# A SwiGLU kernel's first loads in another order: gates of F tiles 2 and 3 ahead of x 256-511, and one F tile of the next tokens run by halves

## The chip, the core and the metric

The kernel runs on one core of a Trainium2 chip. The metric is device time in microseconds (us) of one execution; the kernel before took 115.84 us (median of three runs, 115.55 to 115.91). The engines are named as in the profile: PE is the matrix engine (PEld its weight loads), DVE the vector engine, ACT the scalar engine, POOL the GpSimd engine, and SP the engine that here only issues DMA transfers. The 16 DMA engines move what SP and ACT issue.

## What is computed

```python
B, S, D, F = 1, 2048, 512, 1376          # x: [1, S, D], all bf16

def reference(x, w_gate, w_up, w_down):
    g = _silu(x @ w_gate)
    u = x @ w_up
    return (g * u) @ w_down
```

With S = 2048 tokens, the gate and up products have an inner dimension of 512 (four blocks of 128) and 1376 columns: ten F tiles of 128 and a rest of 96.

## The kernel before

**Tiles and stages.** Tokens are taken in four chunks of 512 (c = 0 to 3; 'tokens 512-1023' are chunk 1), F in tiles of 128 (ft = 0 to 9). Two F tiles make a unit u. A plain gate or up group of one F tile and one chunk is 4 inner blocks of 512 tokens, each a pair of matmuls of 64 weight columns that stand side by side in the array and run together (`gu_emit`, L424); a group of whole chunks is thus 4 pairs. Most units are not done plainly, but by a seven-product scheme (class `Unit`, L610 and L622) on 2 chunks by 2 F tiles, which needs sums of weight blocks (`w_sums`, on POOL, written to ss_sb) and of token blocks (`x_sums`, written to tt_sb: T1 to T4). Ahead of these units, F tiles 0 to 3 of chunk 0 and the first three tiles of `early` (0, 1, 2) of chunk 1 are done plainly. After all of that the down projection runs (L720, L748, L858, L870), again with a seven-product scheme in part.

**The front.** x is needed transposed (inner dimension on the partitions). Tokens 0 to 255 come as plain rows (`xn`) and are transposed on PE (L373, L380); tokens 256 to 511 (`x0b`), 512 to 767 (`x1a`), 768 to 1023 (`x1b`) and later chunks come through transposing DMAs (L279). Weights come in slabs of two F tiles, gate and up apart (L267): `wg0` and `wu0` hold F tiles 0 and 1, `wg2` and `wu2` F tiles 2 and 3. PE starts with matmuls on constants (L350), transposes xn, and then runs, each as soon as its load has landed: the gates of F tiles 0 and 1 on tokens 0-255 (matmuls of 256 columns), the same gates on tokens 256-511, the ups of F tiles 0 and 1, then gates and ups of F tiles 2 and 3 (`classic(0, [2, 3])`, L1012), then `classic(1, [ft])` for F tiles 0, 1, 2 of chunk 1 (L1013). Each finished pair of groups goes through `classic_out`: a silu on ACT (L332) and a product on DVE (L337).

**What sets the order.** All work is recorded in a `Plan`. PE and SP keep the order in which the code records it; ACT, DVE and POOL are ordered by a small list scheduler from durations, lags, priorities and expected landing times written in the code. Each recorded operation waits only on semaphores of what it needs. SP issues the loads one after another into one queue that all 16 DMA engines serve; a load's semaphore counts 16 when all of them have finished their part. The load semaphores named below are s_dma30 = wg0, s_dma22 = x0b, s_dma21 = wu0, s_dma29 = wg2, s_dma20 = wu2, s_dma0 = x1a, s_dma1 = x1b; s_A, s_D, s_G and s_P count finished operations of ACT, DVE, POOL and PE.

**PSUM banks.** Groups take the 8 banks in turn (0, 2, 1, 3, 4, 5, 6, 7). In chunk 0 the first four groups use banks 0 to 3, the next four 4 to 7.

**Two chains beside PE.** The token sums T1 to T4 of chunks 0 and 1 are made on DVE and wait for x1a, x1b and the weight sums of unit 0 on POOL (which need wg0 and wu0). The weight sums of the next units on POOL wait for the last of T1 to T4.

Of the kernel before, what the change touches and what calls it, by code (L numbers as in the profile page):

```python
# [168 lines left out]
def bass_standalone__swiglu_ffn__prompt_kernel(nc, x, w_gate, w_up, w_down, out):  # L169
    _, S, D = x.shape  # L170
    F = w_gate.shape[1]
    P = 128
    KD = D // P
# [4 lines left out]
    SC = 512  # L178
# [6 lines left out]
    HT = SC // 2  # L185
    HC = P // 2
    NXN = HT // P
    NB = 8
# [10 lines left out]
    with ExitStack() as es:  # L199
# [55 lines left out]
        def load(name, emit, writes, busy, lag):  # L255
            nonlocal landed
            landed += lag
            i = take(homes[name] if name in homes else rest[0])
            plan.add("S", emit, writes=writes, busy=busy, lag=1800, dma=(i, 16)).land = landed + (300 if landed < 10000 else 1600)

        slabs = [(0, 2), (2, 4), (4, 6), (6, 8), (8, NFF + 1)]
        slab_of = {ft: a for a, b in slabs for ft in range(a, b)}

        def load_w(name, src, m, c0, f0, f1):
            load(
                name,
                lambda e: e.dma_start(  # L267
                    w_sb[:, :, m, c0:c0 + f1 - f0], src[:, f0:f1].rearrange("(k p) f -> p k f", p=P)
                ),
                [name], 600, 3.7 * (f1 - f0),  # L270
            )

        def load_slab(a, b):
            load_w(f"wg{a}", w_gate, 0, a * P, a * P, min(b * P, F))
            load_w(f"wu{a}", w_up, 1, a * P, a * P, min(b * P, F - 32))

        def load_x(name, t0, t1):
            load(
                name, lambda e: e.dma_start_transpose(xT_sb[:, :, t0:t1], xf[t0:t1, :]), [name], 1500, 4 * (t1 - t0)  # L279
            )  # L280
# [5 lines left out]
            ),  # L286
            ["xn"], 500, 770,
        )
        load_w("wg0", w_gate, 0, 0, 0, slabs[0][1] * P)
        load_x("x0b", HT, SC)  # L290
        load_w("wu0", w_up, 1, 0, 0, slabs[0][1] * P)
        load_slab(*slabs[1])
        for i in range(2):
            load_x(f"x1{'ab'[i]}", SC + i * HT, SC + (i + 1) * HT)
        load_slab(*slabs[2])
# [18 lines left out]
        for i in range(2):  # L314
            load(
                f"wdy{i}",
                lambda e, i=i: e.dma_start(wdt_sb[2 * R * i:2 * R * (i + 1), 0, :], w_down[NFF * P:F - R, :]),
# [12 lines left out]
        def silu_op(out, src, reads, writes, prio=5, busy=A_BUSY):  # L330
            return plan.add(
                "A", lambda e: e.activation(out, src, ACT.Silu), reads, writes, busy, A_LAG, prio  # L332
            )

        def tt_op(engs, out, a, b, alu, reads, writes, prio, busy, after=()):
            return plan.add(
                engs, lambda e: e.tensor_tensor(out, a, b, alu), reads, writes, busy,  # L337
                G_LAG if engs == "G" else D_LAG, prio, after=after,
            )
# [5 lines left out]
        def pe(emit, reads, writes, n, step=PE_STEP, after=()):  # L345
            return plan.add("P", emit, reads, writes, int(n * step), PE_LAG, dma=None, after=after)
# [58 lines left out]
        n_group = 0  # L405

        def next_bank():
            nonlocal n_group
            b = turn[n_group % NB]
            n_group += 1  # L410
            return b

        def x_keys(c):
            if c == 1:
                return ["x1a", "x1b"]
            if c:
                return [f"x{c}"]
            return [("x0a", dk) for dk in range(KD)] + ["x0b"]

        def gu_emit(m, ft, c, b, dks, n0, n1):  # L420
            def emit(e):
                for dk in dks:
                    for h in (0, HC):
                        ins = e.matmul(  # L424
                            psum[h:h + HC, b, n0:n1], lhsT=w_sb[:, dk, m, ft * P + h:ft * P + h + HC],
                            rhs=xT_sb[:, dk, c * SC + n0:c * SC + n1], start=(dk == 0), stop=(dk == KD - 1),
                            tile_position=(0, h),
                        )
                return ins
            return emit  # L430

        def gu_whole(m, ft, c, b):
            def emit(e):
                for dk in range(KD):
                    ins = e.matmul(  # L435
                        bank(b), lhsT=w_sb[:, dk, m, ft * P:(ft + 1) * P], rhs=xT_sb[:, dk, c * SC:(c + 1) * SC],
                        start=(dk == 0), stop=(dk == KD - 1),
                    )
                return ins
            return emit  # L440

        def gu_group(m, ft, c, b, whole=False):
            emit = gu_whole(m, ft, c, b) if whole else gu_emit(m, ft, c, b, range(KD), 0, SC)
            pe(emit, x_keys(c) + [f"w{'gu'[m]}{slab_of[ft]}"], [("b", b)], KD)
# [3 lines left out]
        def ring(name, tiles):  # L448
            n = rings.get(name, 0)
            rings[name] = n + 1  # L450
            i = n % len(tiles)
            return tiles[i][:, :], (name, i)

        def hview(ft, c):
            return (h0_sb, h1_sb)[c // 2][:, ft, c % 2 * SC:(c % 2 + 1) * SC]
# [8 lines left out]
        def classic_out(ft, c, bg, bu):  # L464
            sg, ksg = ring("sg", sg_sb)
            silu_op(sg, bank(bg), [("b", bg)], [ksg])
            tt_op("D", hview(ft, c), sg, bank(bu), ALU.mult, [ksg, ("b", bu)], [("h", ft, c)], 5, D_BUSY)

        def classic(c, fts, own=None):
            gates = [next_bank() for ft in fts] if own is None else own[:1]  # L470
            ups = [next_bank() for ft in fts] if own is None else own[1:]
            for ft, b in zip(fts, gates):
                gu_group(0, ft, c, b, own is not None)
            for ft, b in zip(fts, ups):
                gu_group(1, ft, c, b, own is not None)
            for ft, bg, bu in zip(fts, gates, ups):
                classic_out(ft, c, bg, bu)
# [91 lines left out]
        def x_sums(pi, eng, prio, after):  # L569

            c0, c1 = 2 * pi, 2 * pi + 1
            xk = x_keys(c0) + x_keys(c1)
            key = lambda n, k: ("tt", pi, X_SUM[n], k)
            last, first = after, None
            for n in ("T1", "T2", "T3", "T4"):
                behind = last
                last = []
                for k0, k1 in [(0, KH)] if pi == 0 else [(k, k + 1) for k in range(KH)]:
                    block = lambda k, c: xT_sb[:, k * KH + k0:k * KH + k1, c * SC:(c + 1) * SC]
                    at = lambda n: tt_sb[pi][:, X_SUM[n], k0:k1, :]  # L580
                    rd = lambda n: at(n).bitcast(FP32)
                    B11, B12, B21, B22 = (block(k, c) for k in range(2) for c in (c0, c1))
                    a, b, of_ = {
                        "T1": (B12, B11, ()), "T2": (B22, rd("T1"), ["T1"]),
                        "T3": (B22, B12, ()), "T4": (B21, rd("T2"), ["T2"]),
                    }[n]
                    last.append(tt_op(
                        eng, at(n), a, b, ALU.subtract, xk + [key(o, k) for o in of_ for k in range(k0, k1)],
                        [key(n, k) for k in range(k0, k1)], prio, 1160 if eng == "D" else 1250, behind,
                    ))  # L590
                first = first or last
            for k in range(KH):
                cast_op("A", tt_sb[pi][:, X_SUM["B22"], k, :], xT_sb[:, KH + k, c1 * SC:(c1 + 1) * SC], xk, [key("B22", k)], 8, A_BUSY, first if pi else ())
            return last
# [89 lines left out]
                silu_op(sg, g, [kg], [ksg], 3)  # L684
                tt_op("G", hview(ft, c), sg, v, ALU.mult, [ksg, kv], [("h", ft, c)], 3, 1250, h_free(ft, c))

        g0, u0, g1, u1 = [next_bank() for i in range(4)]
        wkey = [f"wg{slab_of[0]}", f"wu{slab_of[0]}"]
        for dk in range(KD):
            for ft, b in ((0, g0), (1, g1)):  # L690
                pe(gu_emit(0, ft, 0, b, [dk], 0, HT), [("x0a", dk), wkey[0]], [("b", b)], 0.5)
        for ft, b in ((0, g0), (1, g1)):
            pe(gu_emit(0, ft, 0, b, range(KD), HT, SC), ["x0b", wkey[0]], [("b", b)], 2)
        for ft, b in ((0, u0), (1, u1)):
            gu_group(1, ft, 0, b)
        classic_out(0, 0, g0, u0)
        classic_out(1, 0, g1, u1)

        F_ORDER = [ft for u in U_ORDER[1] for ft in (2 * u, 2 * u + 1)]
        LAST_T = NST - 1  # L700
# [308 lines left out]
        units = [(pi, u) for pi in range(2) for u in U_ORDER[pi]]  # L1009
        early = [2 * u + i for u in range(NFF // 2) if u not in U_ORDER[0] for i in range(2)]  # L1010
        sums = w_sums(0, 8, (), "A")
        classic(0, [2, 3])  # L1012
        for ft in early[:3]:  # L1013
            classic(1, [ft])
        sums = x_sums(0, "D", 6, sums)
        for u in U_ORDER[0]:
            sums = w_sums(u, 2, sums, "A")
        sums = x_sums(1, "G", 2, sums)
# [68 lines left out]
```

## Time and profile before

| what | before |
|---|---|
| median of three runs | 115.84 us (115.55 to 115.91) |
| profiled execution, its own time | 115.91 us |
| its span, first to last instruction | 114.6 us |
| PE busy | 110.9 us (97%) |
| DVE, ACT, POOL busy | 76.8, 63.8, 61.5 us |
| granted PE clock | 1.000 |
| HBM read, written | 4.75 MB, 2.10 MB |

The span is the time from the first to the last instruction; the 1.3 us between it and the execution's own time lie outside the program. Matmuls overlap in the array, so a busy PE says little about its pace: the pace is read from the starts of two matmuls. The chain of work that ended last is followed back from the last instruction to what released each step; 'SPq' in it is SP's issuing of a DMA. In a timeline, each row begins with the start and the length in us, and brackets hold the idle time before it and what ended it. In the DMA view a load's row ends with the us from its issue to its landing.

### The profile page before, as it was taken

Reading aid. Unit: us, or ns where it says so; the run is one execution under the profiler, and the core shown is the slowest. Engines: PE = TensorE matmul, PEld = TensorE weight load, DVE = VectorE, ACT = ScalarE, POOL = GpSimd, SP = SyncE. Lnnn points to the kernel's source line nnn. Section 1 sums busy time; section 2 is a strip of 40 time slices with the busy share of each in tenths; the row PEclk is TensorE's granted clock in tenths of the full one; section 3 lists DMA queues with packets and bytes.
Section 4 is the critical chain, followed back from the end, with each engine's and each line's share of the span. In section 5 each row is a group of like instructions: output and inputs, shape, how many; then the busy total and the mean of one; then the engine's idle time right before and its main releaser. Section 6 shows DMA issues by size and latency. Waiting matters only on the chain.

```text
span 114.6 us, 1775 instructions
## 1 busy us (share of the span) xinstructions
PE 110.9 (97%) x652; PEld 70.4 (61%) x660; DVE 76.8 (67%) x113; ACT 63.8 (56%) x123; POOL 61.5 (54%) x57
## 2 busy tenths in 40 slices
PE   7999999999999999999999999999999999999993
PEld 2776566646685857677675858654344556866452
DVE  0113899874866839493957769499999957486423
ACT  5344565874878897767678786740576960000000
POOL 1059003999999999987999999975000000000000
PEclk9999999999999999999999999999999999999999
DMA  2998999995000000000000000000041002227966
GB/s 82 239 273 185 276 259 231 265 361 140 1 0 0 3 0 3 0 0 6 0 0 0 3 0 0 0 0 0 8 135 46 0 0 46 52 46 182 201 195 199
DMA packets 22808, 9.84 MB, mean 86 GB/s; under 512 B 12848, under 2 KB 22672, under 8 KB 22800
## 3 DMA queue, kind: packets, MB, share of 16 engines
q1 hardware_dynamic: 20656, 8.69, 31.6%
q10 hardware_dynamic: 2144, 1.05, 3.2%
q8 instruction: 5, 0.08, 0.3%
q14 instruction: 3, 0.02, 0.1%
HBM read 4.75 MB, written 2.10 MB: 60 GB/s over the span
## 4 chain that ended last, share of the span: by engine, by line
PE 86%; SPq 6%; DMA 4%; issue 1%; DVE 1%
PE psum L610 32%; PE psum L720 15%; PE psum L622 12%; PE psum L858 10%; PE psum L424 5%; DMA xT_sb<-in_x_dram 4%; PE psum L870 4%; SPq L279 4%; PE psum L488 3%; PE psum L748 3%; SPq L267 2%; PE psum L435 2%; PE psum L514 2%; DVE o_sb L326 1%; SPq L284 0%
## 5 line engine op out<-in xcount | busy, mean ns | idle before, releaser
L610 PE MATMUL psum<-tt_sb,ss_sb 128*128 128x512 f32 x160 | 40.0, 402 | 0.0
L610 PEld LDWEIGHTS psum<-tt_sb,ss_sb 128*128 128x128 f32 x160 | 29.9, 188 | 7.5 <-DVE psum L326 0.3
L337 DVE TENSOR_TENSOR ts_sb<-r_sb,psum 128x512 f32<-128x512 f32 x32 | 20.6, 682 | 14.7 <-ACT r_sb L325 14.7
L337 POOL TENSOR_TENSOR h_sb<-sg_sb,ts_sb 128x512 bf16<-128x512 f32 x16 | 20.8, 1302 | 2.8 <-ACT sg_sb L332 2.8
L337 DVE TENSOR_TENSOR h_sb<-sg_sb,psum 128x512 bf16<-128x512 f32 x24 | 16.4, 683 | 6.2 <-PE psum L424 5.8
L325 ACT ACTIVATE r_sb<-psum 128x512 f32<-128x512 f32 x32 | 17.3, 596 | 5.4 <-PE psum L610 5.4
L332 ACT ACTIVATE sg_sb<-psum 128x512 f32<-128x512 f32 x24 | 14.4, 602 | 10.6 <-PE psum L610 5.3
L337 POOL TENSOR_TENSOR ss_sb<-w_sb 128x512 fp32r<-128x512 bf16 x10 | 11.4, 1160 | 13.8 <-DVE tt_sb L337 7.5
L720 PE MATMUL psum<-wd_sb,h_sb 128*128 128x512 bf16 (+2 forms) x98 | 17.9, 336 | 0.2 <-issue 0.2
L622 PE MATMUL psum<-xT_sb,w_sb 128*128 128x512 bf16 x59 | 14.2, 380 | 0.4 <-issue 0.2
L720 PEld LDWEIGHTS psum<-wd_sb,h_sb 128*128 128x128 bf16 x100 | 8.3, 98 | 9.2 <-issue 1.0
L424 PE MATMUL psum<-xT_sb,w_sb 128*64 128x512 bf16 (+1 forms) x128 | 12.9, 362 | 0.2 <-DMA xT_sb<-in_x_dram 0.2
L332 ACT ACTIVATE sg_sb<-ts_sb 128x512 f32<-128x512 f32 x16 | 10.2, 637 | 2.2 <-DVE ts_sb L337 2.2
L424 PEld LDWEIGHTS psum<-xT_sb,w_sb 128*64 128x64 bf16 x128 | 8.4, 114 | 4.3 <-issue 0.7
L622 PEld LDWEIGHTS psum<-xT_sb,w_sb 128*128 128x128 bf16 x64 | 5.5, 98 | 7.9 <-issue 2.5
L326 DVE COPY psum<-psum 128x512 f32<-128x512 f32 x8 | 5.6, 699 | 0.8 <-PE psum L622 0.2
L337 POOL TENSOR_TENSOR ss_sb<-w_sb,ss_sb 128x512 fp32r<-128x512 bf16 x5 | 5.8, 1168 | 0.2
L337 POOL TENSOR_TENSOR ss_sb<-ss_sb,w_sb 128x512 fp32r<-128x512 f32 x5 | 5.8, 1166 | 0.0
L326 DVE CAST o_sb<-psum 128x512 bf16<-128x512 f32 (+2 forms) x6 | 3.0, 512 | 4.2 <-PE psum L720 3.1
L337 POOL TENSOR_TENSOR ss_sb<-wd_sb 128x640 fp32r<-128x640 bf16 x4 | 5.6, 1414 | 0.0
L858 PE MATMUL psum<-tt_sb,ss_sb 128*128 128x512 f32 x20 | 5.6, 418 | 0.0
L858 PE MATMUL psum<-th_sb,ss_sb 128*128 128x512 f32 x20 | 5.5, 411 | 0.0
(72 smaller groups left out, 122.4 us busy)
## 6 DMA issues: line engine op xcount, KB each, us to landing
wd_sb<-in_w_down_dram SPq DMA_DIRECT2D x1, 1280.0 KB, 8.1
w_sb<-in_w_gate_dram SPq DMA_DIRECT2D x4, 256.0 KB, 4.2
w_sb<-in_w_up_dram SPq DMA_DIRECT2D x4, 256.0 KB, 4.3
out_dram<-o_sb SPq DMA_DIRECT2D x7, 128.0 KB, 1.8
out_dram<-xT_sb ACTq DMA_DIRECT2D x4, 128.0 KB, 2.3
out_dram<-xT_sb ACTq DMA_DIRECT2D x2, 256.0 KB, 3.2
w_sb<-in_w_gate_dram SPq DMA_DIRECT2D x1, 352.0 KB, 5.0
w_sb<-in_w_up_dram SPq DMA_DIRECT2D x1, 320.0 KB, 4.3
```

The source lines that it names most:

```text
L279: name, lambda e: e.dma_start_transpose(xT_sb[:, :, t0:t1], xf[t0:t1, :]), [name], 1500, 4 * (t1 - t0)
L325: return e.activation(out, src, ACT.Copy)
L326: return e.tensor_copy(out, src)
L332: "A", lambda e: e.activation(out, src, ACT.Silu), reads, writes, busy, A_LAG, prio
L337: engs, lambda e: e.tensor_tensor(out, a, b, alu), reads, writes, busy,
L424: ins = e.matmul(psum[h:h + HC, b, n0:n1], lhsT=w_sb[:, dk, m, ft * P + h:ft * P + h + HC], rhs=xT_sb[:, dk, c * SC + n0:c * SC + n1], sta ...
L488: ins = e.matmul(psum[m:m + HC, b, :], lhsT=w_sb[:, dk, 0, XC0 + m:XC0 + m + HC], rhs=xT_sb[:, dk, c * SC:(c + 1) * SC], start=(dk == 0), ...
L610: ins = e.matmul(bank(dst), lhsT=s[:, k, :], rhs=t[:, k, :], start=(start and k == 0), stop=(k == KH - 1), skip_group_check=True,)
L622: ins = e.matmul(bank(dst), lhsT=w_sb[:, k0 + k, m, f:f + P], rhs=xT_sb[:, k0 + k, c:c + SC], start=(start and k == 0), stop=(k == KH - 1) ...
L720: ins = e.matmul(psum[:, b, 0:c1 - c0], lhsT=hrows(F_ORDER[n], t, 0, P), rhs=wd_sb[:, F_ORDER[n], c0:c1], start=(start and n == n0), stop= ...
L858: ins = e.matmul(bank(dst), lhsT=self.ds[s][:, j, self.q, :], rhs=self.dt[t][:, j, :], start=(start and n == 0), stop=(n == NFF // 2 - 1), ...
L870: ins = e.matmul(bank(dst), lhsT=wd_sb[:, 2 * j + a, d * P:(d + 1) * P], rhs=h0_sb[:, 2 * j + a, 0:SC], start=(n == 0), stop=(n == NFF // ...
```

## The change

Three things are moved; nothing is computed that was not computed before.

- **Loads.** wg2 is issued right behind wg0, ahead of x0b. The order is xn, wg0, wg2, x0b, wu0, wu2, x1a, x1b, and the same as before from there on.
- **Chunk 0.** Gates of F tiles 0 and 1 on tokens 0-255 as before; then gates of F tiles 2 and 3 on tokens 0-255; then the four gates on tokens 256-511; then the four ups on whole chunks, each followed by its silu and product. Gates take banks 0 to 3, ups 4 to 7. `classic(0, [2, 3])` falls away.
- **Chunk 1.** The first of its three plain F tiles (F tile 0) runs gate and up on tokens 512-767 (needs x1a alone), then both on tokens 768-1023 (needs x1b). The other two are unchanged.

The priority of `x_sums(0, ...)` is 4 instead of 6. In the order that the scheduler makes, all four products of chunk 0 stand ahead of T1 on DVE now, and T2 directly behind T1; before, the fourth product stood between them.

```diff
--- before.py
+++ after.py
@@ -286,10 +286,11 @@
             ),
             ["xn"], 500, 770,
         )
-        load_w("wg0", w_gate, 0, 0, 0, slabs[0][1] * P)
+        for a, b in slabs[:2]:
+            load_w(f"wg{a}", w_gate, 0, a * P, a * P, b * P)
         load_x("x0b", HT, SC)
-        load_w("wu0", w_up, 1, 0, 0, slabs[0][1] * P)
-        load_slab(*slabs[1])
+        for a, b in slabs[:2]:
+            load_w(f"wu{a}", w_up, 1, a * P, a * P, b * P)
         for i in range(2):
             load_x(f"x1{'ab'[i]}", SC + i * HT, SC + (i + 1) * HT)
         load_slab(*slabs[2])
@@ -684,17 +685,20 @@
                 silu_op(sg, g, [kg], [ksg], 3)
                 tt_op("G", hview(ft, c), sg, v, ALU.mult, [ksg, kv], [("h", ft, c)], 3, 1250, h_free(ft, c))
 
-        g0, u0, g1, u1 = [next_bank() for i in range(4)]
-        wkey = [f"wg{slab_of[0]}", f"wu{slab_of[0]}"]
+        first = range(4)
+        gates = [(0, 1, 2, 3)[ft] for ft in first]
+        ups = [NB // 2 + ft for ft in first]
+        n_group = NB
         for dk in range(KD):
-            for ft, b in ((0, g0), (1, g1)):
-                pe(gu_emit(0, ft, 0, b, [dk], 0, HT), [("x0a", dk), wkey[0]], [("b", b)], 0.5)
-        for ft, b in ((0, g0), (1, g1)):
-            pe(gu_emit(0, ft, 0, b, range(KD), HT, SC), ["x0b", wkey[0]], [("b", b)], 2)
-        for ft, b in ((0, u0), (1, u1)):
-            gu_group(1, ft, 0, b)
-        classic_out(0, 0, g0, u0)
-        classic_out(1, 0, g1, u1)
+            for ft in first[:2]:
+                pe(gu_emit(0, ft, 0, gates[ft], [dk], 0, HT), [("x0a", dk), "wg0"], [("b", gates[ft])], 0.5)
+        for ft in first[2:]:
+            pe(gu_emit(0, ft, 0, gates[ft], range(KD), 0, HT), [*x_keys(0)[:KD], "wg2"], [("b", gates[ft])], 2)
+        for ft in first:
+            pe(gu_emit(0, ft, 0, gates[ft], range(KD), HT, SC), ["x0b", f"wg{slab_of[ft]}"], [("b", gates[ft])], 2)
+        for ft in first:
+            gu_group(1, ft, 0, ups[ft])
+            classic_out(ft, 0, gates[ft], ups[ft])
 
         F_ORDER = [ft for u in U_ORDER[1] for ft in (2 * u, 2 * u + 1)]
         LAST_T = NST - 1
@@ -1009,10 +1013,15 @@
         units = [(pi, u) for pi in range(2) for u in U_ORDER[pi]]
         early = [2 * u + i for u in range(NFF // 2) if u not in U_ORDER[0] for i in range(2)]
         sums = w_sums(0, 8, (), "A")
-        classic(0, [2, 3])
-        for ft in early[:3]:
+        g, u = next_bank(), next_bank()
+        for h in range(2):
+            for m, b in ((0, g), (1, u)):
+                emit = gu_emit(m, early[0], 1, b, range(KD), h * HT, (h + 1) * HT)
+                pe(emit, [f"x1{'ab'[h]}", f"w{'gu'[m]}{slab_of[early[0]]}"], [("b", b)], KD / 2)
+        classic_out(early[0], 1, g, u)
+        for ft in early[1:3]:
             classic(1, [ft])
-        sums = x_sums(0, "D", 6, sums)
+        sums = x_sums(0, "D", 4, sums)
         for u in U_ORDER[0]:
             sums = w_sums(u, 2, sums, "A")
         sums = x_sums(1, "G", 2, sums)
```

SP's queue at the start of the program, before and then now (128x4x256 is a weight slab of two F tiles, the first DMA_TRANSPOSE is x0b, the next two x1a and x1b):

```order
L284 DMA xn_sb<-in_x_dram 128x1024
L267 DMA w_sb<-in_w_gate_dram 128x4x256
L279 DMA_TRANSPOSE xT_sb<-in_x_dram 128x4x256
L267 DMA w_sb<-in_w_up_dram 128x4x256
L267 DMA w_sb<-in_w_gate_dram 128x4x256
L267 DMA w_sb<-in_w_up_dram 128x4x256
L279 DMA_TRANSPOSE xT_sb<-in_x_dram 128x4x256 x2
```

```order
L284 DMA xn_sb<-in_x_dram 128x1024
L267 DMA w_sb<-in_w_gate_dram 128x4x256 x2
L279 DMA_TRANSPOSE xT_sb<-in_x_dram 128x4x256
L267 DMA w_sb<-in_w_up_dram 128x4x256 x2
L279 DMA_TRANSPOSE xT_sb<-in_x_dram 128x4x256 x2
```

One gate load has moved from behind wu0 to ahead of x0b; wu0 and wu2 follow x0b.

PE from where the gates of F tiles 0 and 1 on tokens 0-255 are done, to the end of chunk 0 (64x256 is one matmul of a half-chunk pair, 64x512 of a whole-chunk pair), before and now:

```order
L424 MATMUL psum<-xT_sb,w_sb 64x256 [waits s_dma22]
L424 MATMUL psum<-xT_sb,w_sb 64x256 x15
L424 MATMUL psum<-xT_sb,w_sb 64x512 [waits s_dma21]
L424 MATMUL psum<-xT_sb,w_sb 64x512 x15
L424 MATMUL psum<-xT_sb,w_sb 64x512 [waits s_dma29]
L424 MATMUL psum<-xT_sb,w_sb 64x512 x15
L424 MATMUL psum<-xT_sb,w_sb 64x512 [waits s_dma20]
L424 MATMUL psum<-xT_sb,w_sb 64x512 x15
```

```order
L425 MATMUL psum<-xT_sb,w_sb 64x256 [waits s_dma29]
L425 MATMUL psum<-xT_sb,w_sb 64x256 x15
L425 MATMUL psum<-xT_sb,w_sb 64x256 [waits s_dma22]
L425 MATMUL psum<-xT_sb,w_sb 64x256 x31
L425 MATMUL psum<-xT_sb,w_sb 64x512 [waits s_dma21]
L425 MATMUL psum<-xT_sb,w_sb 64x512 x15
L425 MATMUL psum<-xT_sb,w_sb 64x512 [waits s_dma20]
L425 MATMUL psum<-xT_sb,w_sb 64x512 x15
```

Before, PE comes to x0b (s_dma22) first and to wg2 (s_dma29) after wu0 (s_dma21). Now it comes to wg2 first, with 16 matmuls of 256 columns, and then to x0b with 32; the ups follow with 32 of 512 columns.

PE at the first plain F tile of chunk 1, before and now:

```order
L424 MATMUL psum<-xT_sb,w_sb 64x512 [waits s_dma1,s_dma0,s_A]
L424 MATMUL psum<-xT_sb,w_sb 64x512 x7
L424 MATMUL psum<-xT_sb,w_sb 64x512 [waits s_D]
L424 MATMUL psum<-xT_sb,w_sb 64x512 x7
L424 MATMUL psum<-xT_sb,w_sb 64x512 [waits s_A]
```

```order
L425 MATMUL psum<-xT_sb,w_sb 64x256 [waits s_dma0,s_A]
L425 MATMUL psum<-xT_sb,w_sb 64x256 x7
L425 MATMUL psum<-xT_sb,w_sb 64x256 [waits s_A]
L425 MATMUL psum<-xT_sb,w_sb 64x256 x7
L425 MATMUL psum<-xT_sb,w_sb 64x256 [waits s_dma1]
L425 MATMUL psum<-xT_sb,w_sb 64x256 x15
```

Before, the first matmul there waits for x1a and x1b; now it waits for x1a, and x1b is first needed 16 matmuls of 256 columns later.

## The prediction

> **What bounds the kernel now.** I read the page's shares first, then the chain that ended last, then PE's timeline around the one place where that chain is not PE.
>
> ```profile
> PE 110.9 (97%) x652; PEld 70.4 (61%) x660; DVE 76.8 (67%) x113; ACT 63.8 (56%) x123; POOL 61.5 (54%) x57
> PE 86%; SPq 6%; DMA 4%; issue 1%; DVE 1%
> 4.76 2.69 SPq L279
> ...
> 7.49 5.05 DMA xT_sb<-in_x_dram
> 12.55 0.14 issue
> 12.68 5.37 PE psum L424 x48
> ...
> 112.01 0.88 DVE o_sb L326 x3
> ```
>
> The first line is the engines' busy time, the second the chain's shares, the others are pieces of the chain (start, length). From 12.68 us to 112.01 the chain is PE with small "issue" pieces. Ahead of that it is not PE: SP issues x1a (4.76), then x1b (7.49), and x1b lands at 12.55. So whatever PE does up to 12.68 is free, as long as it is done by then; and whatever is taken from the wait for x1b shortens the program, if nothing later takes it back. How long PE waited there is read from starts of matmuls:
>
> ```profile
> 4.92 0.42 PE L424 MATMUL psum<-xT_sb,w_sb 128*64 128x256 bf16 x2
> 6.22 0.40 PE L424 MATMUL psum<-xT_sb,w_sb 128*64 128x256 bf16 x4
> 7.10 0.40 PE L424 MATMUL psum<-xT_sb,w_sb 128*64 128x512 bf16 x2
> 12.06 0.40 PE L424 MATMUL psum<-xT_sb,w_sb 128*64 128x512 bf16 x2
> 12.68 0.62 PE L424 MATMUL psum<-xT_sb,w_sb 128*64 128x512 bf16 x4 [0.22 <-DMA xT_sb<-in_x_dram]
> ```
>
> These come from five narrow windows, one row each. 4.92 is the first gate pair, 6.22 the first pair on tokens 256-511 (x0b), 7.10 the first up pair, 12.06 the last pair of chunk 0, 12.68 the first of chunk 1. From 7.10 to 12.06 there are 23 pairs of 512 columns, so one takes 4.96 / 23 = 0.216. From 6.22 to 7.10 there are 8 pairs of 256 columns, 0.11 each. PE could have begun chunk 1 at 12.06 + 0.216 = 12.28. It began at 12.68: **0.40 us lost**. (The row's idle 0.22 is less, because the last matmuls are still draining.)
>
> **When the loads land.** Issue starts from SP's timeline, then, in the same order, us to landing from windows of the DMA view that hold one issue each:
>
> ```profile
> 1.21 0.41 SPq L267 DMA_DIRECT2D w_sb<-in_w_gate_dram  x1
> 1.67 1.33 SPq L279 DMA_TRANSPOSE xT_sb<-in_x_dram  x1
> 3.04 0.57 SPq L267 DMA_DIRECT2D w_sb<-in_w_up_dram  x1
> 3.66 0.51 SPq L267 DMA_DIRECT2D w_sb<-in_w_gate_dram  x1
> 4.21 0.51 SPq L267 DMA_DIRECT2D w_sb<-in_w_up_dram  x1
> w_sb<-in_w_gate_dram SPq DMA_DIRECT2D x1, 256.0 KB, 3.6
> xT_sb<-in_x_dram SPq DMA_TRANSPOSE x1, 4.3
> w_sb<-in_w_up_dram SPq DMA_DIRECT2D x1, 256.0 KB, 3.9
> w_sb<-in_w_gate_dram SPq DMA_DIRECT2D x1, 256.0 KB, 4.8
> w_sb<-in_w_up_dram SPq DMA_DIRECT2D x1, 256.0 KB, 5.0
> xT_sb<-in_x_dram SPq DMA_TRANSPOSE x1, 5.3
> ```
>
> Issue plus landing: wg0 4.8, x0b 6.0, wu0 6.9, wg2 8.5, wu2 9.2, x1a 4.76 + 5.3 = 10.1, x1b 12.55. They land in the order of issue, 0.7 to 1.5 us apart, only x1b 2.5 behind x1a. Between a landing and the first matmul that needs it lie 12.68 - 12.55 = 0.13 us.
>
> **The change, part by part.**
>
> *x1b.* Chunk 0 has the same columns as before, so without a new wait PE reaches chunk 1 at 12.28 plus the price of the split (next). It needs x1a at that time; x1a landed at 10.1. The half of F tile 0 on tokens 512-767 is 8 pairs of 256, 8 x 0.11 = 0.88 us, so x1b is needed at about 12.31 + 0.88 - 0.13 = 13.06; it landed at 12.55. Its issue stays where it was: ahead of x1a stand the same six issues with the same lengths. Gain 0.40, with 0.5 us to spare.
>
> *The split.* Gates of F tiles 2 and 3, 8 pairs of 512, become 16 of 256; F tile 0 of chunk 1 the same. 32 x 0.11 - 16 x 0.216 = 0.06 by the rounded rows; by half that (0.109 a pair) it is 0.03. I take 0.05. Weight loads are as many as matmuls and double too; the 0.11 was measured with them.
>
> *wg2 earlier.* PE needs it at 6.22, when the 8 pairs on tokens 0-255 of F tiles 0 and 1 are through. Right behind wg0 it lands about 4.8 + 0.9 = 5.7 (0.9 is what wu0 took behind x0b), at worst 4.8 + 1.5 = 6.3 (what it took itself). Need 6.22 - 0.13 = 6.09. Taken at no cost; 0.2 at worst.
>
> *x0b later.* This is the tight place. PE works 8 pairs of 256 on F tiles 2 and 3 from 6.22 to 7.10, so x0b must land by 6.97. Behind wg2 it lands at 6.0 + 0.9 = 6.9, with the gate load's interval of 1.5 at 7.5, and earlier than 6.9 if its own slow stretch does not come with it:
>
> ```profile
> 4.00:5.00 1.00, 1.00 (x23) 0.86 (x19) 0.51 (x2) 0.80 (x3) 0.00 (x0) 1.00 1.18 150
> 6.00:7.00 1.00, 1.00 (x23) 1.00 (x21) 0.00 (x0) 0.12 (x1) 0.00 (x0) 1.00 1.17 283
> ```
>
> The last figure is GB/s: while x0b moved (4 to 5 us) the DMA engines were as busy as in 6 to 7, but moved half as much. At the later rate x0b would land about 0.4 earlier, 6.5. So its wait lies between 0 and 0.5; I take 0, the nearest row (wu0's interval) giving 6.9.
>
> [...]
>
> *wu0 and wu2.* wu0 lands one load later, 6.9 + 0.9 = 7.8 or at wg2's old time 8.5; PE needs it after 16 pairs of gates on tokens 256-511, 7.10 + 16 x 0.11 - 0.13 = 8.73. wu2 keeps its place, 9.2, need about 10.5. Both free.
>
> *DVE and POOL.*
>
> ```profile
> 7.04 2.27 POOL L337 TENSOR_TENSOR ss_sb<-w_sb 128x512 fp32r<-128x512 bf16 x2 [5.97 <-DMA w_sb<-in_w_up_dram]
> 10.50 1.17 POOL L337 TENSOR_TENSOR ss_sb<-w_sb,ss_sb 128x512 fp32r<-128x512 bf16 x1
> 19.17 1.16 POOL L337 TENSOR_TENSOR ss_sb<-w_sb 128x512 fp32r<-128x512 bf16 x1 [7.51 <-DVE tt_sb L337]
> 12.67 1.23 DVE L337 TENSOR_TENSOR tt_sb<-xT_sb 128x1024 fp32r<-128x1024 bf16 x1 [0.28 <-DMA xT_sb<-in_x_dram]
> 13.81 0.68 DVE L337 TENSOR_TENSOR h_sb<-sg_sb,psum 128x512 bf16<-128x512 f32 x1
> 17.87 1.22 DVE L337 TENSOR_TENSOR tt_sb<-xT_sb,tt_sb 128x1024 fp32r<-128x1024 bf16 x1
> 42.80 2.29 POOL L337 TENSOR_TENSOR tt_sb<-xT_sb 128x512 fp32r<-128x512 bf16 x2
> 45.30 0.76 PEld L610 LDWEIGHTS psum<-tt_sb,ss_sb 128*128 128x128 f32 x4 [0.32 <-DVE psum L326]
> ```
>
> POOL's four sums of unit 0 start with wu0 and take 11.67 - 7.04 = 4.6; now 7.9 to 12.5. DVE ran T1 to T4 and three products from 12.67 to 19.09 without a pause, 6.4 us. Now the product of F tile 3 comes first, when its up is done at about 12.5; T1 then starts at 13.1, behind POOL's 12.5 and x1b's 12.55. The same seven operations from 12.5 end at 18.9, and POOL's next sums start at 19.0 instead of 19.17. PE comes 0.35 earlier to everything POOL makes, POOL 0.1 to 0.2 earlier. The nearest need is T3 of the second pair of chunks, ready at 45.09; PE uses it behind the four loads of the last row, which end at 46.06, so more than 0.9 us later; 0.2 of that goes. The short wait at 45.30 for a copy on DVE is relative to PE's own pace and stays.
>
> *Sum.* 0.40 gained, 0.05 paid: the profiled execution of 115.91 (span 114.6 and 1.3 outside it) becomes 115.56. It stands 0.07 above the median of 115.84, so against the median **115.5**.
>
> **The rivals.**
>
> *x0b a little late.* At 7.1 to 7.3 PE waits 0.1 to 0.3, and 115.6 to 115.8 is left. Against it: the DMA engines have data all the time, and x0b's slow stretch has room to shrink. For it: my margin is 0.07.
>
> *x0b late enough to lose (the other side).* One mechanism: PE stands at 7.10 until x0b is there. From a landing at 6.97 + 0.35 = 7.3 on, the wait eats the gain; from 7.7 on the kernel is measurably slower. With x0b slow as in 4 to 5 us, behind a gate load that took 1.5 as wg2 did, plus a straggling DMA engine, it lands at 7.5 to 8.2: waits of 0.5 to 1.2, times 116.0 to 116.7.
>
> *A fetch of instructions in the way.*
>
> ```profile
> q8 instruction: 5, 0.08, 0.3%
> q8 instruction: 1, 0.02, 13.2%
> ```
>
> The page has five such packets, so 16 KB each; the second row is the window 10.0 to 10.5, just where x1b lands late: 13.2% of 16 engines for 0.5 us, so one DMA engine was held for 1.06 us. As a load counts only when all 16 engines are through, that is how x1b's extra 1.5 can arise. The change adds 32 matmuls and 32 weight loads by about 14 us, so if PE is the one that fetches, the fetch comes earlier: half of the added instructions lie ahead of 8.9, and at PE's pace of 4 instructions in 0.216 us that is some 1.7 us, near 8.7. Then x1a would land at up to 11.6 (need 12.2), still free. If it comes earlier still and holds wu2, that lands at 9.2 + 1.5 = 10.7 against a need of 10.5: a wait of 0.2, 115.7.
>
> [...]
>
> [...]
>
> **How the numbers follow.** What a measurement of this kernel can tell from no change is about 0.3%, 0.35 us; the forecast lies just at that edge. Chances: everything in time, 115.35 to 115.65, 0.45; x0b a little late or wu2 held, 115.6 to 115.85, 0.27; wait moved, 115.9, 0.08; x0b or wg2 clearly late, 116.0 to 116.7, 0.20. Faster by over 0.3%: most of the first, 0.40. Slower: 0.22. Same: 0.38. The range goes from 115.25 (0.40 won, a split at no cost, and 0.2 for the spread of the three runs) to 116.2, which leaves out the worse half of the last case.
>
> **What would show it.** In the profile after, the chain should be PE from about 5 us on, with no DMA piece; the first pair on tokens 256-511 at 7.1, the first up pair at 8.86, the first pair of chunk 1 at 12.3 and no idle time before it. A wait on xT_sb's DMA near 7 us, its length the loss, shows x0b late. A wait at 6.2 shows wg2. POOL's second set of sums should start near 19.0. I am wrong if PE's starts are as forecast but the end is not earlier: then a wait behind 20 us, on POOL or DVE, has taken it back.

## The result, and the profile after

| kernel | median | range | executions |
|---|---|---|---|
| before | 115.81 us | 115.55 to 116.18 | 18 |
| after | 115.45 us | 115.09 to 115.92 | 18 |

The ratio is **0.9969, 95% interval 0.9957 to 0.9982**: 0.36 us less, 0.21 to 0.50. The forecast was 115.5.

The profiled execution of the changed kernel is one of those 18, and with 115.92 us the longest of them, as long as the profiled one of before (115.91). So its trace shows what the changed kernel can lose, not what it gains. First its page's busy shares and shares of the chain, then pieces of its chain (start, length):

```profile
PE 111.6 (97%) x692; PEld 69.9 (61%) x692; DVE 77.0 (67%) x113; ACT 63.6 (55%) x123; POOL 61.5 (54%) x57
PE 90%; DMA 4%; SPq 3%; DVE 1%; issue 0%
```

```profile
2.20 1.68 SPq L279
...
3.93 4.85 DMA w_sb<-in_w_up_dram
8.78 0.04 issue
8.83 8.84 PE psum L425 x96
...
20.26 0.13 issue
20.39 1.99 PE psum L489 x16
```

In the chain of before, PE took over at 12.68, behind the landing of x1b. Here PE takes over at 8.83, behind the landing of wu0 (8.78), and has no pause at the start of chunk 1. The new pause is at 20.39. The starts on PE, from its timeline, are to be held against the rows of before: first pair, first up pair, first pair of chunk 1, first whole-chunk matmul of unit 0:

```profile
4.79 0.43 PE L425 MATMUL psum<-xT_sb,w_sb 128*64 128x256 bf16 x2
8.83 0.41 PE L425 MATMUL psum<-xT_sb,w_sb 128*64 128x512 bf16 x2 [0.17 <-DMA w_sb<-in_w_up_dram]
12.31 0.39 PE L425 MATMUL psum<-xT_sb,w_sb 128*64 128x256 bf16 x4
24.05 0.38 PE L436 MATMUL psum<-xT_sb,w_sb 128*128 128x512 bf16 x1
```

Chunk 1 begins at 12.31 instead of 12.68, 0.37 earlier. But the first whole-chunk matmul of unit 0 (the 24.05 row) began at 24.04 before: the 0.37 are gone again by then. DVE's and POOL's timelines show where:

```profile
13.70 1.22 DVE L338 TENSOR_TENSOR tt_sb<-xT_sb 128x1024 fp32r<-128x1024 bf16 x1 [0.43 <-POOL ss_sb L338]
...
18.43 1.22 DVE L338 TENSOR_TENSOR tt_sb<-xT_sb,tt_sb 128x1024 fp32r<-128x1024 bf16 x1
19.56 0.68 DVE L338 TENSOR_TENSOR h_sb<-sg_sb,psum 128x512 bf16<-128x512 f32 x1
```

```profile
8.93 2.27 POOL L338 TENSOR_TENSOR ss_sb<-w_sb 128x512 fp32r<-128x512 bf16 x2 [7.86 <-DMA w_sb<-in_w_up_dram]
...
12.40 1.17 POOL L338 TENSOR_TENSOR ss_sb<-w_sb,ss_sb 128x512 fp32r<-128x512 bf16 x1
19.73 2.28 POOL L338 TENSOR_TENSOR ss_sb<-w_sb 128x512 fp32r<-128x512 bf16 x2 [6.16 <-DVE tt_sb L338]
```

The pause at 20.39 ends one chain. wu0 lands at 8.78, POOL's four sums end at 12.40 + 1.17 = 13.57, T1 on DVE starts at 13.70 instead of 12.67, T4 at 18.43, and the product of the third tile of chunk 1, behind T4 on DVE, ends at 19.56 + 0.68 = 20.24. (It stood behind T4 before, too, and ended at 19.69 there, well ahead of the need at 20.45.) It frees the PSUM bank that the group at L489 needs: PE's wait for DVE's count ends behind it, at 20.34, and the group's first weight load begins at 20.36. That group could have begun at 20.10 (the L515 groups began at 19.23, and take 8 x 0.109); it began at 20.39, 0.29 later.

The merged row of the chain hides a second wait right behind. The other half of these 16 matmuls is on the last chunk of tokens, x3, and begins with this row of PE's weight loads:

```profile
21.33 0.14 PEld L489 LDWEIGHTS psum<-xT_sb,w_sb 128*64 128x64 bf16 x4 [0.36 <-DMA xT_sb<-in_x_dram]
```

x3 landed at 21.29 (20.52 before). At PE's pace this half would have begun at 20.39 + 8 x 0.108 = 21.26, so x3 cost 0.07 more: 0.36 in all. But without the pause at 20.39 it would have been wanted at 20.97, and x3 alone would have held PE until 21.33. So the 0.29 is not a price: take away the wait for the bank, and the 0.36 are lost to x3 alone.

The loads, SP's issue and then the landing in the DMA view (x1a, then x1b):

```profile
5.11 2.38 SPq L279 DMA_TRANSPOSE xT_sb<-in_x_dram  x1
7.53 2.01 SPq L279 DMA_TRANSPOSE xT_sb<-in_x_dram  x1
```

```profile
xT_sb<-in_x_dram SPq DMA_TRANSPOSE x1, 7.0
...
xT_sb<-in_x_dram SPq DMA_TRANSPOSE x1, 5.5
```

x1a landed at 12.1 (before: 10.1), x1b at 13.0 (12.55). Whole, F tile 0 would have waited at 12.31 here.

**How to turn a place in the trace into time.** The start of chunk 1 plus 103.2 us is an execution's own time wherever nothing waits behind it: 12.68 + 103.23 = 115.91 in the profile of before, and 103.18 to 103.26 in nine of the profiles below (the others: 103.07 and 103.14 in after_free and before_wu0_x0, and 103.43 in whole23, which waits at 21.34). The changed kernel's one above has 103.61; the difference is mostly the 0.36. If other executions are like the profiled ones, the front decides, and a median of 115.81 means a chunk 1 that begins near 12.6, a median of 115.45 one near 12.25.

### The profile page after: what moved, and what is told of

Same layout as the page of the kernel before. It is cut to its first block, busy times and chain, and to the rows that moved or that the text cites. A ratio compares the mean times of both kernels' runs of the same rounds, so it can differ in the third digit from the quotient of the medians.

```text
span 114.6 us, 1847 instructions
## 1 busy us (share of the span) xinstructions
PE 111.6 (97%) x692; PEld 69.9 (61%) x692; DVE 77.0 (67%) x113; ACT 63.6 (55%) x123; POOL 61.5 (54%) x57
## 4 chain that ended last, share of the span: by engine, by line
PE 90%; DMA 4%; SPq 3%; DVE 1%; issue 0%
PE psum L611 32%; PE psum L724 15%; PE psum L623 12%; PE psum L862 10%; PE psum L425 8%; DMA w_sb<-in_w_up_dram 4%; PE psum L874 4%; PE psum L489 3%; PE psum L752 3%; PE psum L515 2%; PE psum L436 2%; SPq L279 1%; SPq L267 1%; DVE o_sb L327 1%; SPq L284 0%
## 5 line engine op out<-in xcount | busy, mean ns | idle before, releaser
L724 PE MATMUL psum<-wd_sb,h_sb 128*128 128x512 bf16 (+2 forms) x100 | 18.4, 337 | 0.0
L623 PE MATMUL psum<-xT_sb,w_sb 128*128 128x512 bf16 x64 | 15.4, 381 | 0.0
L425 PE MATMUL psum<-xT_sb,w_sb 128*64 128x256 bf16 (+1 forms) x160 | 12.7, 319 | 0.2 <-DMA w_sb<-in_w_up_dram 0.2
```

Source lines behind the costliest of these rows:

```text
L425: ins = e.matmul(psum[h:h + HC, b, n0:n1], lhsT=w_sb[:, dk, m, ft * P + h:ft * P + h + HC], rhs=xT_sb[:, dk, c * SC + n0:c * SC + n1], sta ...
L623: ins = e.matmul(bank(dst), lhsT=w_sb[:, k0 + k, m, f:f + P], rhs=xT_sb[:, k0 + k, c:c + SC], start=(start and k == 0), stop=(k == KH - 1) ...
L724: ins = e.matmul(psum[:, b, 0:c1 - c0], lhsT=hrows(F_ORDER[n], t, 0, P), rhs=wd_sb[:, F_ORDER[n], c0:c1], start=(start and n == n0), stop= ...
```

## The experiments

Each time is a median; each ratio is to the kernel before on the same chip, whose median was 115.63, 115.72, 115.75 and 115.71 us in the four sets.

**Set 1: the parts apart.** The kernel before with only F tile 0 of chunk 1 by halves (halves_only), and the changed kernel without it (no_halves):

```diff
 # halves_only, in before; no_halves is the reverse, in after
-        for ft in early[:3]:
+        g, u = next_bank(), next_bank()
+        for h in range(2):
+            for m, b in ((0, g), (1, u)):
+                emit = gu_emit(m, early[0], 1, b, range(KD), h * HT, (h + 1) * HT)
+                pe(emit, [f"x1{'ab'[h]}", f"w{'gu'[m]}{slab_of[early[0]]}"], [("b", b)], KD / 2)
+        classic_out(early[0], 1, g, u)
+        for ft in early[1:3]:
             classic(1, [ft])
```

> Before, with F tile 0 of chunk 1 run by halves and nothing else changed. My theory (the gain is the wait for x1b that falls away): 0.3 to 0.4 us faster, 115.4 to 115.5, as much as the whole change, and in the profile PE goes from chunk 0 to chunk 1 without idle time at about 12.3. Rival (the gain is the other order of loads and gates, which lets PE run on whatever has landed): no difference, 115.8.

Measured: 115.40, ratio 0.9988 (0.9970 to 1.0006). No gain that can be told from none, though the interval reaches to 0.35 us less, which is what the forecast leaves after the price of the split. In its profiled execution (115.74) the first eight pairs of gates all ran at half pace (0.213 us each, for 0.109), and PE reached chunk 1 only at 12.52, with x1b there since 12.16. That execution would not have waited for x1b without the halves either.

> The changed kernel with F tile 0 of chunk 1 run whole, so that it waits for x1a and x1b at once; loads and chunk 0 in the changed order. My theory: PE waits for x1b again, until 12.6 to 13.2 in the profile, and the time is 115.8 or up to 0.4 us slower. Rival (loads and gates make the gain): 115.4 to 115.5.

Measured: 115.23, **ratio 0.9964 (0.9944 to 0.9983)**: the whole gain of the changed kernel, without the halves. My theory, that the halves are what makes this gain, falls here. Its profiled execution alone, with 116.28 the longest of 13 (the next is 115.56), waited at the start of chunk 1, by 0.34 against PE's pace:

```profile
13.04 0.62 PE L425 MATMUL psum<-xT_sb,w_sb 128*64 128x512 bf16 x4 [0.18 <-DMA xT_sb<-in_x_dram]
```

The third kernel of the set goes at the 16 KB fetch that lies beside the straggling x1b (10.41 in the profile of before): F tiles 2 and 3 of chunk 0 with matmuls of 128 weight columns, half as many. If the fetch is PE's, it comes later then.

```diff
-        classic(0, [2, 3])
+        classic(0, [2, 3], whole=True)   # gu_whole in place of gu_emit
```

> Before, with gates and ups of F tiles 2 and 3 of chunk 0 done by matmuls of 128 weight columns in place of pairs of 64: the same PE time, 16 matmuls and 16 weight loads fewer by 12.3 us, and no change of order. Theory (the 16 KB fetch is PE's and holds one DMA engine, which makes x1b late): the fetch comes 1 to 2 us later than 10.4, x1b lands near 11.0 on all engines, the wait at 12.3 is gone, 115.4 to 115.5. Rival (the fetch is not PE's, or x1b is late for another reason): fetch at 10.4, x1b at 12.5, 115.8.

Measured: 115.89, ratio 1.0015 (0.9996 to 1.0034). Its trace, by the DMA view of 13.8 to 14.8 us, by x1b's issue and landing, and by the chain:

```profile
q8 instruction: 1, 0.02, 6.0%
```

```profile
6.88 1.66 SPq L279 DMA_TRANSPOSE xT_sb<-in_x_dram  x1
```

```profile
xT_sb<-in_x_dram SPq DMA_TRANSPOSE x1, 3.6
```

```profile
4.92 4.06 PE psum L424 x48
8.98 3.56 PE psum L435 x16
12.54 5.30 PE psum L424 x48
...
21.30 0.04 issue
21.34 1.05 PE psum L488 x8
```

The one 16 KB packet of q8 has moved behind 13.8 us (10.41 before), and x1b lands at 6.88 + 3.6 = 10.5, 3.6 us from its issue for 5.05 before. So the fetch moves with PE's instruction count (here 16 matmuls and 16 weight loads fewer), and with the fetch gone from 10.4 the late part of x1b is gone. Yet with x1b 1.8 us ahead of its need (12.3) the kernel is not faster. Two costs are in the trace: each switch between 64- and 128-column matmuls takes 0.1 (the steps at 8.91 and 12.47 are 0.31 instead of 0.216), and a wait of 0.2 for x3 at 21.34. They are of the size of what was to be won, so this run alone decides nothing on the wait.

The changed kernel again, for another execution's trace:

> The changed kernel once more, for a second profile. Its first profile was of its slowest execution (115.92), with PE waiting for wu0 until 8.8 and for x256-... bank 5 near 20.3. If these waits are what sets a slow execution apart, a faster one (115.1 to 115.5) shows them shorter; if both profiles show the same waits at different times, something else varies.

Measured: 115.59 in one execution. PE timeline:

```profile
4.47 1.06 PE L425 MATMUL psum<-xT_sb,w_sb 128*64 128x256 bf16 x16
6.12 7.09 PE L425 MATMUL psum<-xT_sb,w_sb 128*64 128x256 bf16 x92 [0.58 <-DMA w_sb<-in_w_gate_dram]
```

wg2, which I had costed at nothing, is waited for: the eight first pairs were done by 4.47 + 8 x 0.109 = 5.34, and the next began at 6.12, 0.77 later; x0b then cost 0.15 more. Nothing waited behind it.

**Set 2: what the wait for x1b is worth.** F tile 0 of chunk 1 is computed from chunk 0's tokens, so that x1a and x1b are needed 1.73 us later and nothing else changes: in the kernel before (before_x0), and in the changed one without halves (no_halves_x0).

```diff
-        for ft in early[:3]:
+        g, u = next_bank(), next_bank()
+        gu_group(0, early[0], 0, g)
+        gu_group(1, early[0], 0, u)
+        classic_out(early[0], 1, g, u)
+        for ft in early[1:3]:
             classic(1, [ft])
```

> The kernel before, but F tile 0 of tokens 512-1023 is computed from tokens 0-511, which are in place: its part of the output is not the reference's. x1a and x1b are then needed eight pairs of 512 columns per projection later, 16 x 0.108 = 1.73 us, and the wait for x1b (0.40 us in the profile) is gone without any change of a load, an order or a count of instructions. If that wait stands in ordinary executions as in the profiled one, the time falls by 0.3 to 0.4, to 115.3 on a chip where the kernel before takes 115.65. The rival: in ordinary executions x1b lands earlier than in the profiled one, the wait is 0.1 or less, and the time stays within 0.1 of the kernel before; then the changed kernel's gain has to come from the front of the program, not from this wait.

Measured: 115.69, **ratio 0.9995 (0.9970 to 1.0021)**. Without the wait for x1b the kernel before is not measurably faster; a gain of 0.40 lies outside the interval, one of 0.3 does not. Its trace shows another wait in the place, for wu0 ahead of the first up pair, 0.42 against PE's pace:

```profile
7.28 1.05 PE L424 MATMUL psum<-xT_sb,w_sb 128*64 128x512 bf16 x8 [0.25 <-DMA w_sb<-in_w_up_dram]
```

> The changed kernel with F tile 0 of tokens 512-1023 whole, and computed from tokens 0-511 as in before_x0 (so that part of the output is not the reference's). Its profile as no_halves showed a wait of 0.34 us for x1b (landed 12.91). If ordinary executions have that wait too, this kernel is 0.3 faster than no_halves was against the kernel before (0.42 less), so about 0.7 below it. If they have not, it stays at 0.4 below, as no_halves. My theory after the first runs: the new order of loads lets the gates begin in good time and no wait for x1b stands in most executions, so 0.4 below, and the halves of the changed kernel buy nothing.

Measured: 115.46, ratio 0.9963 (0.9942 to 0.9984): the same as no_halves and as the changed kernel. With the new order nothing is seen of a wait for x1b either, halves or none.

Does an earlier fetch alone gain? The ups of F tiles 0 and 1 in halves of 256 columns, in the kernel before, add 16 matmuls and 16 weight loads ahead of 9 us:

```diff
-            gu_group(1, ft, 0, b)
+            for h in range(2):
+                pe(gu_emit(1, ft, 0, b, range(KD), h * HT, (h + 1) * HT), x_keys(0) + [wkey[1]], [("b", b)], 2)
```

> The kernel before, with the ups of F tiles 0 and 1 of tokens 0-511 in halves of 256 columns: 16 matmuls and 16 weight loads more, ahead of 9 us, nothing else moved. If PE's instruction fetch sits where PE's count puts it, it comes some 0.9 us earlier (9.5 for 10.41) and x1b's straggling part is gone or smaller. If the fetch alone makes the wait for x1b, this kernel gains 0.2 to 0.4, less some 0.03 for the split. If a fetch ahead of x1a's packets delays all of x1a and x1b instead, as the changed kernel's trace suggests, x1b lands at 12.2 to 13.0 and the time is within 0.15 of the kernel before.

Measured: 115.70, ratio 0.9991 (0.9970 to 1.0012). The fetch came at 8.96. First SP's issue of x1a and of x1b, then the us from issue to landing of each:

```profile
4.75 2.16 SPq L279 DMA_TRANSPOSE xT_sb<-in_x_dram  x1
...
6.95 1.57 SPq L279 DMA_TRANSPOSE xT_sb<-in_x_dram  x1
```

```profile
xT_sb<-in_x_dram SPq DMA_TRANSPOSE x1, 6.2
...
xT_sb<-in_x_dram SPq DMA_TRANSPOSE x1, 5.0
```

x1a lands at 10.9 instead of 10.1, x1b at 11.95 instead of 12.55, with its 16 parts together. The delay has moved from x1b to x1a, and the time did not follow.

The changed kernel once more, beside these:

> The changed kernel once more, beside the others on one chip: 0.36 below the kernel before by its first comparison (interval 0.21 to 0.50). If the halves buy nothing it equals no_halves_x0 within 0.1; if both it and no_halves_x0 are free of the wait for x1b, they differ by the 0.3 us that the changed kernel's first profile lost at 20.4 us, behind a copy on DVE, where that loss stands in ordinary executions.

Measured: 115.49, ratio 0.9964 (0.9941 to 0.9986). Its profiled execution is a short one, 115.29, and its chain is the one that I had forecast: PE from the start, no DMA in it.

```profile
4.39 0.53 PE psum L398 x10
4.92 12.51 PE psum L425 x160
17.43 1.73 PE psum L489 x16
19.16 0.86 PE psum L515 x8
20.02 1.73 PE psum L489 x16
```

wu0 landed at 7.70 here, POOL's second sums began at 18.97, x3 landed at 19.85, and neither wait of 20.4 and 21.3 is there. That agrees with the chain from wu0 to the pause at 20.39; one execution with everything earlier does not prove it.

**Set 3: do two waits stand in for each other?** In before_x0 the wait for wu0 had taken the place of that for x1b. So the need for wu0 is taken away, alone (before_wu0) and with the need for x1b (before_wu0_x0, which has before_x0's edit too):

```diff
         for ft, b in ((0, u0), (1, u1)):
-            gu_group(1, ft, 0, b)
+            gu_group(0, ft, 0, b)
```

> The kernel before, with the ups of F tiles 0 and 1 of tokens 0-511 computed from the gate weights, which are in place (so that part of the output is not the reference's): wu0, the third load behind the first 256 tokens, is not needed there. No load, order or count changes. In before_x0's profile PE waited 0.42 us for wu0's last part (7.23) at the first up pair. Theory A, that in the kernel before wu0 and x1b are each the last to come in a part of the executions, so that either wait takes the other's place: within 0.15 of the kernel before. Theory B, wu0 alone is what the old order loses: 0.3 to 0.4 less. Theory C, no wait for a load loses it: 0.

Measured: 115.73, ratio 1.0008 (0.9991 to 1.0025). In its trace x1b is waited for in place of wu0, 0.54 against PE's pace:

```profile
12.52 0.84 PE L424 MATMUL psum<-xT_sb,w_sb 128*64 128x512 bf16 x6 [0.38 <-DMA xT_sb<-in_x_dram]
```

> Both needs taken from the kernel before: the ups of F tiles 0 and 1 from the gate weights, and F tile 0 of tokens 512-1023 from tokens 0-511 (two parts of the output are not the reference's). Theory A: 0.3 to 0.5 less than the kernel before, though neither alone pays. Theory B: the same as before_wu0, 0.3 to 0.4 less. Theory C: no change, and the loss of the old order lies behind 17 us, on DVE or POOL.

Measured: 115.33, **ratio 0.9975 (0.9958 to 0.9992)**. The four corners, as ratios to the kernel before:

| | x1b needed at the start of chunk 1 | needed 1.73 us later |
|---|---|---|
| wu0 needed at the first ups | 1 | 0.9995 (0.9970 to 1.0021) |
| not needed there | 1.0008 (0.9991 to 1.0025) | 0.9975 (0.9958 to 0.9992) |

Neither wait alone is worth anything that can be told from nothing; both together are worth 0.29 us (0.09 to 0.49). Theory A, that either wait takes the other's place, fits best. With wu0's need gone, x1b's is worth something: 115.73 against 115.33 in the same set. The reverse, that wu0's need adds anything once x1b's is gone, is not separated from noise (0.9995 and 0.9975, with intervals that overlap), so Theory A is likely and not proven.

Which part of the new order removes them? x0b_first puts x0b ahead of wg2 again and runs the gates of F tiles 2 and 3 whole, behind those of F tiles 0 and 1; four gates before four ups stay.

```diff
-        for a, b in slabs[:2]:
-            load_w(f"wg{a}", w_gate, 0, a * P, a * P, b * P)
+        load_w("wg0", w_gate, 0, 0, 0, slabs[0][1] * P)
         load_x("x0b", HT, SC)
+        load_w(f"wg{slabs[1][0]}", w_gate, 0, slabs[1][0] * P, slabs[1][0] * P, slabs[1][1] * P)
...
-        for ft in first[2:]:
-            pe(gu_emit(0, ft, 0, gates[ft], range(KD), 0, HT), [*x_keys(0)[:KD], "wg2"], [("b", gates[ft])], 2)
-        for ft in first:
+        for ft in first[:2]:
             pe(gu_emit(0, ft, 0, gates[ft], range(KD), HT, SC), ["x0b", f"wg{slab_of[ft]}"], [("b", gates[ft])], 2)
+        for ft in first[2:]:
+            gu_group(0, ft, 0, gates[ft])
```

> The changed kernel with one part undone: x0b loads ahead of wg2 again, and F tiles 2 and 3 run their gates whole, behind both token halves of F tiles 0 and 1; then four ups; F tile 0 of tokens 512-1023 whole. Against the kernel before only wu0 and wg2 have changed places, as loads and as work. If the gain is from the third load being a gate load that straggles no less than wu0 did, nothing is gained: within 0.1 of the kernel before. If it is from running gates ahead of ups (ups later, four gate products ready early for ACT), the gain of 0.35 stays. If it is from x0b being third, loaded without a straggling part (five profiles of the changed order show x0b's 16 parts within 0.03 us of each other), it is lost.

Measured: 115.75, ratio 1.0003 (0.9987 to 1.0018). Nothing is left of the gain. So it comes from wg2 ahead of x0b with the work on the first 256 tokens that this allows, not from gates before ups, and not from the halves. The order of the loads and the order of the work were undone together here; which of them counts for how much is not tested.

**Set 4: what the changed kernel still waits for.** All gates of F tiles 0 to 3 on tokens 0-511 are taken from tokens 0-255 and the weights of F tiles 0 and 1; wg2 is then not needed there, and x0b first at the ups, near 8.6.

```diff
-            pe(gu_emit(0, ft, 0, gates[ft], range(KD), 0, HT), [*x_keys(0)[:KD], "wg2"], ...
+            pe(gu_emit(0, ft, 0, gates[ft], range(KD), 0, HT, 0, 2), [*x_keys(0)[:KD], "wg0"], ...   # weights of ft - 2
-            pe(gu_emit(0, ft, 0, gates[ft], range(KD), HT, SC), ["x0b", f"wg{slab_of[ft]}"], ...
+            pe(gu_emit(0, ft, 0, gates[ft], range(KD), HT, SC, HT, 2 * (ft // 2)), [*x_keys(0)[:KD], "wg0"], ...   # tokens 0-255
```

> The changed kernel with the two needs ahead of 8 us taken away: all gates of F tiles 0 to 3 on tokens 0-511 are computed from tokens 0-255 and from the weights of F tiles 0 and 1 (so those parts of the output are not the reference's). Loads, order and counts stay; wg2 is needed no more there and x0b only at the first up pair, near 8.6. If the changed order has no wait left in ordinary executions, as the equality of the changed kernel (0.9964 and 0.9969) with the kernel before less both waits (0.9975) says, the time is that of the changed kernel, 0.3 to 0.4 below the kernel before. If wg2 and x0b are still waited for (0.77 and 0.15 us in the second look at the changed kernel), it is 0.5 to 0.8 below, and that difference is what my prediction's free loads cost.

Measured: 115.15, ratio 0.9949 (0.9921 to 0.9976). The changed kernel's 0.9964 and 0.9969 lie inside that interval. The middle values differ by some 0.2 us, which would be what wg2 and x0b still cost; the runs don't separate it from nothing.

## Why the prediction was right, and where it was not

The time was right: 115.45 for 115.5, and faster, near the edge of what can be told. That was luck, for the reason given was wrong: 0.40 for a wait and the 0.36 that another part of the change gained are of one size by chance.

**The step that failed is "x1b ... Gain 0.40"**, with the sentence it rests on: whatever is taken from the wait for x1b shortens the program, if nothing *later* takes it back. Nothing later had to. PE stood for 0.40 behind x1b in the execution of the profile. In that of before_x0 it stood for 0.42 behind wu0 instead, and in that of halves_only the slow first gates alone took it to 12.52. How often each of these comes last, no run shows. The edit named as the gain, the halves, gave 0.9988 (0.9970 to 1.0006) alone, and leaving it out of the changed kernel cost nothing (0.9964). Removing the need outright gave 0.9995 (0.9970 to 1.0021). What gained is the part that the prediction costed at nothing or as a risk: wg2 ahead of x0b.

**The sum** came out in the profile up to chunk 1: forecast 12.3, measured 12.31, with no wait at that place. The agreement is chance: PE's first gates were earlier and faster than before (4.79 for 4.92, two slow pairs for four), and a wait of 0.34 for wu0 that the sum did not have took that back. The halves mattered in this execution, as x1b landed at 13.0. But that is one execution, 115.92, and the medians it does not explain.

**x0b, the tight place**: forecast to land at 6.9 and needed at 6.97; it landed at 6.68 in the profile, and cost 0.02. The rival "x0b a little late" had 0.15 in after_again.

**wg2** "taken at no cost; 0.2 at worst": right in the first profile, 0.77 in after_again. The need was sized by before's slow start of the gates. In after_again PE was there at 5.34, 0.9 earlier than the 6.22 of before: half of that from an earlier first pair (4.47 for 4.92), half from first pairs at full pace.

**wu0** "free, at worst 8.5": it landed at 8.78, and PE lost 0.34 ahead of the first up pair. Its last part was late (at 8.78, 0.62 behind the one before it), a case that the prediction allowed x1b and x0b but not wu0.

**The wait moved** (115.9 among the chances, a wait of 0.4 for x1b) did not come in the profile: SP issued x1a and x1b from 5.11 on in 4.43 us (from 4.76 on in 4.29 before), x1b landed at 13.0, and the first pair on its tokens began at 13.18, 0.11 behind the pair ahead of it. What sets the length of these issues, no run shows.

**DVE and POOL.** The forecast was that nothing near needs them before T3 at 45.09. It missed the third product of chunk 1 behind T4, which frees a bank that PE wants at 20.10, and the landing of x3 at 21.29, of which it says nothing. POOL's second sums began at 19.73 for a forecast of 19.0. In after_b, with wu0 at 7.70, they began at 18.97. So the 19.0 was right where wu0 was in time.

**The fetch** was forecast near 8.7, and lay at 9.89, 9.20 and 9.31 in the three profiles of the changed kernel. Whose it is, left open there, whole23 shows: it moves with PE's instruction count (behind 13.8 there, 10.41 in before, 8.96 in ups_split). PE's own stream shows nothing of it (in the profile of before its pairs stay 0.216 apart from 10.3 to 11.6); the loads do (x1b's last part 1.5 us behind the one before it in before, or x1a 0.8 later in ups_split). In ups_split, which moves the fetch, the time did not change; whole23 moves it too, but has costs of its own.

**What stays open.** Why the new order takes away both waits. Third behind the first rows of x stands x0b instead of a weight load. In six profiles with x0b third it landed between 6.3 and 7.25 (mean 6.77); in eight with a weight load third, that landed between 6.7 and 7.3 (mean 7.03). From there to chunk 1 lies as much work (24 pairs of 0.216, or 16 of 0.109 and 16 of 0.216: 5.2 us in both). If that load were what PE waits for, 0.26 of the 0.36 would follow; but the two groups overlap, these are profiled executions alone, and in most of them PE did not wait for it. The parts of the load differ more: x0b's last part came at most 0.03 behind the one before it, wu0's 0.34 to 0.57 behind in three of seven. That is a candidate, and not shown. For x1b the profiles show no such thing: in the new order it lands no earlier (11.9 to 13.0; in the old one 12.0 to 12.55, whole23 apart). Yet no_halves at 115.23 must begin chunk 1 near 12.0, so x1b must be there by then in about half of its executions. What loads do in executions other than the profiled ones, no run shows.

## What to carry to other kernels

A wait in one profile is a price only if no other wait, or slow start, ends near it: where two loads are each just too late, removing either may gain nothing. Take away the need, not the load (compute from data that is in place), one at a time and together; that takes four kernels, and enough executions that the differences stand clear of the noise, which here they barely do. And before believing a term of the sum, compare the profiled execution with the spread of the others: that of before, from which the sum was made, was the longest of the three known then, and that of the changed kernel the longest of 18.

## What the runs showed that was not expected

- **The pace of the first gates varies between executions, by up to 0.8 us in all.** The first pairs of 256 columns come 0.213 apart, the others 0.109: in the profile of after the first 2 pairs, in after_b 4, in x0b_first 7, in halves_only and no_halves 8, in after_again and before_x0 none, although the granted clock reads 1.000 in every profile. What makes the first ones slow, and sets their number, no run shows. x0b_first shows what it means. Its chain is PE alone too, and it took 115.69:

```profile
4.42 0.53 PE psum L398 x10
4.96 12.84 PE psum L425 x128
17.80 1.73 PE psum L489 x16
```

The same columns took 12.51 in after_b's chain. An execution that starts at the slow pace needs its loads later, and so can hide the waits that another execution shows.

- **A fetch of 16 KB goes with late loads, in two ways.** Where it began behind x1a's landing (9.88 to 10.41 us, seven profiles), one of x1b's 16 parts came 1.5 us behind the others. Where it began ahead of it (8.96 to 9.91, six profiles), x1a landed 0.8 to 2.0 us later than the 10.1 of before, in four of them with all parts but one late; in after_b x1b was late instead, 2.5 behind x1a.
- **A switch between matmuls of 64 and of 128 weight columns** costs 0.1 us each way (whole23: 0.31 from start to start for 0.216, at 8.91 and at 12.47).
